# Linear attention block with a gated feed-forward: pairing the transposes of the normalized queries, and the attention product in single PSUM banks

## The chip, the core and the metric
One core of a Trainium2 chip runs the whole program in one launch. The metric is the device time in microseconds (us). In three runs the kernel before took 1098.07, 1098.07 and 1098.23 us, median 1098.07 us. The core has TensorE (PE), which multiplies matrices and writes to PSUM, VectorE (DVE), ScalarE (ACT) and GpSimd (POOL), and a queue of SyncE (SP) that issues all transfers of this kernel. PSUM has eight banks. Every engine works through its own list of instructions in order.

## What is computed
```
xn  = layernorm(x)                            # x: 2048 tokens x 576
qkv = xn @ wqkv                               # 32 heads of 18
phi(t) = where(t > 0, t + 1, exp(t)) + 1e-6
kv  = sum over tokens of phi(k)^T v           # per head
z   = sum over tokens of phi(k)
o   = (phi(q) @ kv) / (phi(q) . z + 1e-6)
s   = o @ wo
g   = silu(gelu(xn @ w1 + b1) @ w2 + b2)      # 576 -> 4608 -> 576
out = x + s * g
```
All in float32; the kernel splits operands into a high and a low part (names ending in h and l) and multiplies high by high, high by low and low by high.

## The kernel before, in words
The 2048 tokens are 16 tiles of 128. A first stage makes keys and values of each tile and sums the state. A second stage, which the change touches, makes the attention output of each tile. A third and much longer stage is the feed-forward network (L1148, L1287, L1403).

At the start of the second stage `fold_wo` multiplies the state by `wo` (L708), so that one 576 x 576 matrix, `kw_h` and `kw_l`, takes normalized queries to s. Then a loop, `for i in range(1, NT + 4)` at L1070, is a pipeline over tiles. Iteration i holds, in this order:

- `query(i)`: 28 matmuls into a pair of banks `pq` (`project`, L313).
- `phi_query(i)`: three passes on ACT (L326, L328, L330) and one on DVE (L332), the last reader of `pq`.
- `transpose_p(i - 2)`: five transposes of the normalized queries of tile i - 2 from `pbuf` into a pair of banks `ptp` (L771), then the high part `th` by ACT (L775) and the low parts `tl` and the end of `th` by DVE (L776, L777).
- `pad(i - 1)`: ACT fills the last columns of `pbuf` (L763).
- `beside(i, 2)`: work for the next stage, in some iterations, on ACT, DVE and SP.
- `normalize(i)`: POOL multiplies by the key sums (L741), more `beside` work, then DVE sums by head (L749 to L753), and POOL writes `pbuf` (L754).
- `attend(i - 4)`: 28 matmuls of `th` and `tl` with `kw` into `ps_s` (L789), a copy to SBUF by ACT (L794) and a store.

From i = 16 on there are no queries; in iterations 17 and 18 `beside` prepares the first weights of the next stage (`z.split`, L486 and L487; `w.hi`, `w.lo`, `w.T`, L859 to L875).

PSUM is shared by two pools. `bank2` hands out three pairs of banks in turn (its pool at L53), `bank1` two single banks in turn (L54). Whoever takes a place in turn waits until the last reader of the tile that held it is done. Before the change `pq`, `ptp` and `ps_s` each take a pair in each iteration, and the single banks serve the transposes and the state of the first stage, `ps_kw` of `fold_wo` and, in the third stage, `a` and `e`.

The whole first and second stages stand under `in_order` (L59): on each engine the instructions run in the order in which this program writes them, and no scheduler moves them. So an instruction that waits holds up everything behind it on its engine.

Of the kernel before, what the change touches and what calls it, by code (L numbers as in the profile page):

```python
# [17 lines left out]
D = 576  # L18
HD = 288
F = 4608  # L20
H = 32
DH = 18
NT = S // P
# [21 lines left out]
def linear_attention_gated_ffn(ctx, tc, x, xT, wqkv, wo, w1, w1e, b1, w2, b2, out):  # L45
    nc = tc.nc
# [31 lines left out]
    def stage(cols, name):  # L78
        t = stg.tile([P, D], F32, tag="stg", name=name)
        return t[:, :cols]  # L80

    def bank2(name):
        return psum.tile([P, 2, 512], F32, tag="pp", name=name)

    def bank1(name):
        return psum1.tile([P, 512], F32, tag="p1", name=name)

    def as2(ap):
        return ap.rearrange("p (a b) -> p a b", a=2)
# [233 lines left out]
    def phi_steps(pool, ps, name, out):  # L323

        e = pool.tile([P, D], F32, tag="e", name=f"e{name}")
        nc.scalar.activation(as2(e), ps[:, :, :HD], AF.Relu, scale=-1.0)  # L326
        yield
        nc.scalar.activation(e, e, AF.Exp, scale=-1.0)  # L328
        yield
        nc.scalar.activation(e, e, AF.Identity, bias=tiny[:, 0:1])  # L330
        r = pool.tile([P, D], F32, tag="phi", name=f"phi{name}")
        nc.vector.scalar_tensor_tensor(  # L332
            as2(r), ps[:, :, :HD], 1.000001, as2(e), op0=ADD, op1=ALU.max
        )
        out += [r, e]
# [177 lines left out]
    def query(t):  # L513
        pq[t] = bank2(f"pq{t}")
        project(t, wq_h, wq_l, pq[t])
# [168 lines left out]
    kw_h = kwp.tile([P, KT, D], F32R, name="kw_h")  # L684
    kw_l = kwp.tile([P, KT, D], F32R, name="kw_l")
    p_bufs = []
    for i in range(2):
        p_bufs.append(t2.tile([P, KT * P], F32, name=f"pbuf{i}", bufs=1))

    krs = []  # L690
# [40 lines left out]
    def split_kw(k, elo):  # L731
        split_w(krs[k], k, kw_h, kw_l, elo)
# [3 lines left out]
    def phi_query(t):  # L736
        phi_q[t] = phi(t2, pq.pop(t), f"q{t}")

    def by_sums(t):
        q_t, e = phi_q[t]  # L740
        nc.gpsimd.tensor_tensor(e, q_t, zb, op=MUL)  # L741

    def normalize(t):
        if t:
            by_sums(t)
            beside(t, 0)
        q_t, e = phi_q.pop(t)
        den = t2.tile([P, 2, H], F32, tag="den", name=f"den{t}")
        nc.vector.tensor_reduce(  # L749
            den[:, 0, :], e.rearrange("p (h d) -> p h d", h=H), axis=mybir.AxisListType.X, op=ADD  # L750
        )
        nc.vector.tensor_scalar_add(den[:, 0, :], den[:, 0, :], 1e-6)
        nc.vector.reciprocal(den[:, 1, :], den[:, 0, :])  # L753
        nc.gpsimd.tensor_tensor(  # L754
            p_bufs[t % 2][:, :D].rearrange("p (h d) -> p h d", h=H),
            q_t.rearrange("p (h d) -> p h d", h=H),
            den[:, 1, :, None].to_broadcast([P, H, DH]),
            op=MUL,
        )

    def pad(t):
        pb = p_bufs[t % 2]
        nc.scalar.copy(pb[:, D:], pb[:, 512:D])  # L763

    pT = {}

    def transpose_p(t):
        pb = p_bufs[t % 2]
        pt = bank2(f"ptp{t}").rearrange("p a b -> p (a b)")
        for k in range(KT):  # L770
            nc.tensor.transpose(pt[:, k * P : (k + 1) * P], pb[:, k * P : (k + 1) * P], ident)  # L771
        th = t2.tile([P, KT, P], F32R, tag="th", name=f"th{t}", bufs=3)
        tl = t2.tile([P, KT - 1, P], F32R, tag="tl", name=f"tl{t}", bufs=3)
        p3 = pt[:, : KT * P].rearrange("p (k c) -> p k c", k=KT)
        nc.scalar.copy(th, p3)  # L775
        nc.vector.tensor_tensor(tl, p3[:, :4, :], th[:, :4, :].bitcast(F32), op=SUB)  # L776
        nc.vector.tensor_tensor(th[64:, 4, :], p3[64:, 4, :], th[64:, 4, :].bitcast(F32), op=SUB)  # L777
        pT[t] = (th, tl)

    def attend(t):  # L780
        th, tl = pT.pop(t)
        ps = bank2(f"ps_s{t}")
        seq = []
        for k in range(4):
            seq += [(th, kw_h, k), (th, kw_l, k), (tl, kw_h, k)]
        seq += [(th, kw_h, 4), (th, kw_l, 4)]
        for i, (st, w, k) in enumerate(seq):
            for h in range(2):
                nc.tensor.matmul(  # L789
                    ps[:, h, :HD], st[:, k, :], w[:, k, h * HD : (h + 1) * HD],  # L790
                    start=(i == 0), stop=(i == len(seq) - 1),
                )
        s_sb = stage(D, f"s{t}")
        nc.scalar.copy(as2(s_sb), ps[:, :, :HD])  # L794
        nc.sync.dma_start(s_dram[t], s_sb)

    def hi_lo(pool, shape, tag, bufs, name):
# [217 lines left out]
    def beside(i, k):  # L1015

        if k == 0:
            if i == 3:
                split_kw(3, nc.vector)
            if i == 4:  # L1020
                xsum[0] = XSums(0, tmp_w1)
            if i == 5:
                xsum[1] = XSums(2, lambda name: as2(kw_pair(name).rearrange("p a d -> p (a d)")[:, :1024]))
            sums(i)
            if i in RESTS:
                half, what, *k = RESTS[i]
                if half not in rests:
                    rests[half] = Rest(half)
                getattr(rests[half], what)(*k)
        else:  # L1030
            if i == 16:
                sums(i)
            if i == 17:
                z = xsum[1]
                z.split(z.u, z.s3, nc.vector)
            if i in SPLITS:
                half, n = SPLITS[i]
                z = xsum[half]
                if i in (8, 12):
                    z.place(not half)  # L1040
                z.split(z.u if n == 3 else z.t, getattr(z, f"s{n}"), nc.vector)
                if not half:
                    spill(i - 8)
            if i == 12:
                w2_raw0.append(load_w2_raw(0))
                w1t[0] = W1(0)
            if i == 13:
                w1t[1] = W1(1)
            if i == 16:
                load_we(0)  # L1050
                z = xsum[1]
                rests["x"] = load_rests(1)
                for n, t in ((2, z.h0), (6, z.tiles[0]), (4, z.h1)):
                    load_rest(1, REST_AT[n], 1, t[:, 4])
            if i == 17:
                w = w1t[0]
                w.hi("a"), w.lo("a")
                for j in (5, 6, 7, 4):
                    w.T(j)
                w.hi(6), w.lo(6)  # L1060
            if i == 18:
                load_we(1)
                w = w1t[0]
                for j in ("c", "d"):
                    w.hi(j), w.lo(j)
# [4 lines left out]
    for i in range(1, NT + 4):  # L1070
        if 1 < i < NT:
            query(i)
        if i in X_STORES:
            at, src = X_STORES[i]
            nc.sync.dma_start(x_dram[:, at : at + src.shape[1]], src.bitcast(F32))
        if i == 1:
            phi_query(0)
            nc.scalar.copy(as2(zb), zb_ps[:, :, :HD])
            by_sums(0)
            groups, made = fold_wo(), []  # L1080
            next(groups)
            steps = phi_steps(t2, pq.pop(1), "q1", made)
            next(steps)
            next(groups)
            next(steps)
            next(groups)
            next(steps, None)
            phi_q[1] = made
            next(groups), next(groups)
            normalize(0)  # L1090
            for _ in groups:
                pass
            pad(0)
        for k in {2: (0, 1), 3: (2,)}.get(i, ()):
            split_kw(k, nc.vector)
        if 1 < i < NT:
            phi_query(i)
        if 2 <= i < NT + 2:
            transpose_p(i - 2)
        if 2 <= i < NT + 1:  # L1100
            pad(i - 1)
        beside(i, 2)
        if i < NT:
            normalize(i)
        if i >= 4:
            attend(i - 4)
# [405 lines left out]
    for step in range(n_chunks):  # L1512
# [3 lines left out]
        h = HOps(c)  # L1516
# [142 lines left out]
```

## Time and profile before
| what | value |
|---|---|
| median of three runs | 1098.07 us |
| the profiled execution | 1098.02 us |
| its span, first to last instruction | 1096.3 us |
| second stage, from the first `query` to the first `a` of the third | about 144.6 to 282.4 us |
| busy share of the span: PE, DVE, ACT, POOL | 99%, 75%, 45%, 43% |

All times in the views are counted from the start of the span. In a timeline row stand the start, the duration, the engine, the line, the operation, what is written from what is read, and in brackets the idle time of the engine just before it with what ended it. In the chain of waits stand the start, the duration and what ran, and the times there are up to 0.2 us later than the starts in the timeline, as it goes by ends. Names are shown without buffer numbers, so `pq` is the queries of any tile.

### The profile page before, as it was taken

The numbers are of one execution on the slowest core, as the hardware profiler recorded it, in microseconds if no ns is written. First come the engines' busy times: TensorE is split into PE (matmuls) and PEld (weight loads), VectorE is DVE, ScalarE is ACT, GpSimd is POOL, SyncE is SP. The second block draws the span as 40 slices with busy tenths as digits, with TensorE's granted clock in tenths as the row PEclk, the third lists the DMA queues.
The fourth block names the chain that finished last, engine by engine and source line by source line (L and its number), as shares of the span: only waits on it lengthen the run. The fifth ranks groups of instructions, "written<-read, shape, count | busy, mean of one in ns | idle before, by whom it ended". The sixth has DMA issues, their size and how long they took to land.

```text
span 1096.3 us, 18084 instructions
## 1 busy us (share of the span) xinstructions
PE 1088.6 (99%) x6702; PEld 1008.5 (92%) x6702; DVE 825.6 (75%) x1132; ACT 490.9 (45%) x844; POOL 472.7 (43%) x403
## 2 busy tenths in 40 slices
PE   9999999999999999999999999999999999999998
PEld 8999989999898998989989989899898998998987
DVE  7785748888798888888888888667476584664856
ACT  6454655555545354454453544524224233242352
POOL 4667444323546446464555553424234143242340
PEclk9999999999999999999999999999999999999999
DMA  7999834675959559486585779978676676766352
GB/s 248 269 262 280 311 135 160 205 242 188 342 214 344 190 211 332 152 317 233 187 330 167 287 239 405 387 249 296 210 245 217 204 236 217 229 222 228 122 181 87
DMA packets 88400, 262.54 MB, mean 239 GB/s; under 512 B 11894, under 2 KB 24182, under 8 KB 85624
## 3 DMA queue, kind: packets, MB, share of 16 engines
q1 hardware_dynamic: 88312, 261.38, 70.1%
q8 instruction: 53, 0.87, 0.3%
q14 instruction: 35, 0.29, 0.1%
HBM read 164.24 MB, written 95.17 MB: 237 GB/s over the span
## 4 chain that ended last, share of the span: by engine, by line
PE 99%; DVE 1%; issue 0%; POOL 0%; ACT 0%; DVEq 0%; POOLq 0%
PE pm L1287 35%; PE a L1148 10%; PE e L1148 10%; PE zy L1148 10%; PE pk L313 6%; PE pq L313 5%; PE ps_s L789 5%; PE b L1148 5%; PE pv L313 4%; PE pd L1403 2%; PE ps_kva L382 1%; PE ptp L771 1%; PE ps_kw L708 1%; PE warm L361 0%; PE ps_kvb L382 0%
## 5 line engine op out<-in xcount | busy, mean ns | idle before, releaser
L1293 DVE TENSOR_TENSOR macc<-pm,macc 128x576 f32<-128x576 f32 x218 | 163.8, 752 | 51.9 <-PE pm L1287 50.3
L813 ACT CAST h_h<-g 128x512 fp32r<-128x512 f32 x204 | 121.7, 621 | 133.9 <-PE pm L1287 132.8
L816 DVE TENSOR_TENSOR h_l<-g,h_h 128x512 fp32r<-128x512 f32 x204 | 161.7, 800 | 0.0
L1253 POOL TENSOR_TENSOR mid<-g 128x512 f32<-128x512 f32 x34 | 44.0, 1293 | 105.4 <-ACT g L1156 105.4
L1247 POOL TENSOR_TENSOR g<-g 128x512 f32<-128x512 f32 x34 | 54.9, 1615 | 49.4 <-DVE h_l L816 28.4
L1156 ACT ACTIVATE g<-b,b1c 128x512 f32<-128x512 f32 x36 | 24.8, 689 | 101.9 <-DVE b L1174 101.9
L1165 ACT COPY mid<-a 128x512 f32<-128x512 f32 x36 | 21.1, 585 | 96.4 <-PE a L1148 96.4
L859 POOL TENSOR_TENSOR w1raw<-w1raw 128x256 f32<-128x256 f32 x18 | 13.3, 737 | 116.7 <-ACT h_h L813 68.2
L1168 DVE TENSOR_TENSOR mid<-b,mid 128x512 f32<-128x512 f32 x36 | 24.8, 690 | 46.3 <-PE b L1148 43.0
L1375 POOL TENSOR_TENSOR fin1l<-fin1h,fin1l 128x288 f32<-128x288 f32 x8 | 6.4, 806 | 119.6 <-DMA fin1l<-s_dram 62.9
L1250 POOL TENSOR_TENSOR g<-g 128x512 f32<-128x512 f32 x34 | 55.2, 1623 | 2.7
L1148 PE MATMUL a<-h0r,wa 128*128 128x512 f32 x144 | 50.4, 390 | 0.0
L1148 PE MATMUL a<-xh,wa 128*128 128x512 f32 x144 | 50.4, 390 | 0.0
L816 DVE TENSOR_TENSOR h_l<-mid,h_h 128x512 fp32r<-128x512 f32 x34 | 48.8, 1437 | 1.2
L1156 ACT ACTIVATE g<-e,b1c 128x512 f32<-128x512 f32 x36 | 24.8, 689 | 51.5 <-DVE e L1181 51.5
L754 POOL TENSOR_TENSOR pbuf<-phiq,den 128x576 f32<-128x576 f32 x16 | 19.4, 1214 | 63.9 <-DVE den L753 63.9
L1244 POOL TENSOR_TENSOR g<-g 128x512 f32<-128x512 f32 x34 | 44.2, 1299 | 2.7
L1181 DVE TENSOR_TENSOR e<-e,mid 128x512 f32<-128x512 f32 x36 | 24.8, 689 | 21.5 <-PE e L1148 21.5
L1171 DVE TENSOR_TENSOR mid<-zy,mid 128x512 f32<-128x512 f32 x36 | 24.9, 691 | 19.5 <-PE zy L1148 19.5
L313 PE MATMUL pk<-wkv_h,xh 128*128 128x288 f32 (+1 forms) x160 | 38.1, 320 | 0.5 <-DVE xh L245 0.5
L313 PE MATMUL pk<-wkv_l,xh 128*128 128x288 f32 (+1 forms) x160 | 38.2, 321 | 0.0
L1174 DVE TENSOR_TENSOR b<-e,mid 128x512 f32<-128x512 f32 x36 | 25.2, 699 | 17.2 <-PE e L1148 16.2
(857 smaller groups left out, 3644.4 us busy)
## 6 DMA issues: line engine op xcount, KB each, us to landing
we<-we_dram SPq DMA_DIRECT2D x36, 448.0 KB
w2raw<-w SPq DMA_DIRECT2D x10, 1152.0 KB
op<-w2o SPq DMA_DIRECT2D x18, 576.0 KB
w1raw<-w SPq DMA_DIRECT2D x18, 512.0 KB
op_a<-wa SPq DMA_DIRECT2D x18, 512.0 KB
op_c<-wc SPq DMA_DIRECT2D x18, 512.0 KB
op_d<-wd SPq DMA_DIRECT2D x18, 512.0 KB
wc<-op_c SPq DMA_DIRECT2D x18, 512.0 KB
```

What stands on the lines that cost most here:

```text
L313: nc.tensor.matmul(ps[:, h, : ws.stop - ws.start], st, w[:, k, ws], start=(begin and i == 0), stop=(end and i == len(seq) - 1), skip_group ...
L789: nc.tensor.matmul(ps[:, h, :HD], st[:, k, :], w[:, k, h * HD : (h + 1) * HD], start=(i == 0), stop=(i == len(seq) - 1),)
L813: nc.scalar.copy(pair[0], src)
L816: eng.tensor_tensor(pair[1], src, pair[0].bitcast(F32), op=SUB)
L1148: nc.tensor.matmul(ps, st, mv, start=first and n == 0, stop=n == len(seq) - 1, skip_group_check=True,)
L1156: nc.scalar.activation(g, ps, AF.Gelu_apprx_tanh, bias=b1c[:, f : f + 1])
L1244: tt(src[5, pr], A(1, 0), A(1, 1), op=ADD)
L1247: tt(src[6, pr], src[5, pr], A(0, 0), op=SUB)
L1250: tt(src[3, pr], A(0, 1), src[6, pr], op=SUB)
L1253: tt(src[7, pr], A(0, 0), A(1, 0), op=SUB)
L1287: nc.tensor.matmul(ps[:, q, :HD], hs[p][st][:, cs], m[:, p, :], start=(n == 0 and i not in CHAIN), stop=(n == 5), skip_group_check=True,)
L1293: nc.vector.tensor_tensor(dst, src, dst, op=ADD)
```

## The change
The transposes move: instead of one tile in every iteration from 2 to 17, two tiles, i - 3 and i - 2, in every odd iteration from 3 to 17. Since a `pbuf` may now be held one iteration longer there are three of them instead of two. The product of `attend` goes into the two single banks, one for each half of the columns, for all tiles but the last, which takes a pair as before. Its copy to SBUF is two copies of 288 columns in place of one of 576.

```diff
-    for i in range(2):
+    for i in range(3):
         p_bufs.append(t2.tile([P, KT * P], F32, name=f"pbuf{i}", bufs=1))
...
-            p_bufs[t % 2][:, :D].rearrange("p (h d) -> p h d", h=H),
+            p_bufs[t % 3][:, :D].rearrange("p (h d) -> p h d", h=H),
...
     def attend(t):
         th, tl = pT.pop(t)
-        ps = bank2(f"ps_s{t}")
+        if t < NT - 1:
+            ps = [bank1(f"ps_s{t}{h}")[:, :HD] for h in range(2)]
+        else:
+
+            both = bank2(f"ps_s{t}")
+            ps = [both[:, h, :HD] for h in range(2)]
...
                 nc.tensor.matmul(
-                    ps[:, h, :HD], st[:, k, :], w[:, k, h * HD : (h + 1) * HD],
+                    ps[h], st[:, k, :], w[:, k, h * HD : (h + 1) * HD],
                     start=(i == 0), stop=(i == len(seq) - 1),
                 )
         s_sb = stage(D, f"s{t}")
-        nc.scalar.copy(as2(s_sb), ps[:, :, :HD])
+        for h in range(2):
+            nc.scalar.copy(s_sb[:, h * HD : (h + 1) * HD], ps[h])
         nc.sync.dma_start(s_dram[t], s_sb)
...
-        if 2 <= i < NT + 2:
-            transpose_p(i - 2)
+        if i % 2 and 3 <= i < NT + 2:
+
+            transpose_p(i - 3), transpose_p(i - 2)
         if 2 <= i < NT + 1:
             pad(i - 1)
```

More of the change, by code (lines that the diff above doesn't have):

```diff
@@ L761, in pad @@
     def pad(t):
-        pb = p_bufs[t % 2]
+        pb = p_bufs[t % 3]
         nc.scalar.copy(pb[:, D:], pb[:, 512:D])
@@ L767, in transpose_p @@
     def transpose_p(t):
-        pb = p_bufs[t % 2]
+        pb = p_bufs[t % 3]
         pt = bank2(f"ptp{t}").rearrange("p a b -> p (a b)")
```

## Prediction
> **What bounds the kernel now.** I read the page first, then busy time by stretch, the waits of PE, and the chain of waits.
>
> ```profile
> PE   9999999999999999999999999999999999999998
> ...
> PEclk9999999999999999999999999999999999999999
> ```
>
> ```profile
> 178.30:258.40 80.10, 80.10 (x612) 80.10 (x611) 66.92 (x95) 42.68 (x71) 27.01 (x22) 1.00 0.60 195
> ...
> 282.40:1096.30 813.90, 808.23 (x4814) 737.63 (x4812) 613.28 (x812) 334.78 (x561) 339.70 (x268) 1.00 0.69 242
> ```
>
> ```profile
> PE warm L361 <- POOL ident masks.py:199: 1.5, 1, 1.5
> PE pk L313 <- DVE xh L245: 0.5, 1, 0.5
> PE e L1148 <- DVE b L1174: 0.3, 1, 0.3
> ```
>
> In the page's 40 slices of 27.4 us PE falls under nine tenths only in the last, and the granted clock is full in all. In a stretch's row the first two numbers are its length and PE's busy time. In the middle of the second stage PE is busy for all of 80.10 us, DVE (third busy figure) for 66.92, ACT for 42.68. The waits of PE (its weight loads aside) are three in the whole span, none in the second stage, and one of 0.3 us in the third. PE is idle for 5.7 of the third stage's 813.90 us, and a last slice of eight tenths holds about 5.5 of that: the tail. So time lost by PE in the second stage is not won back: the third stage starts later by as much and has no idle PE time to absorb it. The question is only whether PE does less work, or waits where it did not.
>
> ```profile
> 1.45 4.53 PE warm L361 x20
> 7.58 3.96 PE pk L313 x28
> ...
> 174.13 0.55 PE ptp L771 x5
> 174.68 3.83 PE ps_s L789 x28
> ...
> 186.51 3.73 PE pq L313 x28
> ...
> 194.52 3.73 PE pq L313 x28
> ...
> 271.41 11.20 PE ps_s L789 x84
> ```
>
> One iteration is 194.52 - 186.51 = 8.01 us: 28 matmuls of 3.73, five transposes, 28 matmuls of `attend` of 3.73 (11.20 / 3), so 0.55 for the transposes.
>
> **Part 1: the transposes in tens.** Work on PE is the same: 80 transposes, 896 matmuls. What could go is the change-over between transposes and matmuls.
>
> ```profile
> 169.50 0.71 PE L771 MATMUL ptp<-ident,pbuf 128*128 128x128 f32 x5
> ```
>
> ```profile
> L771 PE MATMUL ptp<-ident,pbuf 128*128 128x128 f32 x80 | 11.3, 272 | 0.0
> ```
>
> One transpose lasts 0.272, five overlapped 0.71, so they follow each other every (0.71 - 0.27) / 4 = 0.11 us, and five make 0.55: all of the iteration's 0.55. The change-over costs nothing within these roundings (0.01). With eight joints fewer the gain lies between 0 and 0.1 us; I take 0.
>
> **Part 2: the first query after a pair waits.** The pairs of banks go in turn. Before, a round is pq, ptp, ps_s. After, the start runs pq2, pq3, ptp0, ptp1, pq4, with three pairs: pq4 gets the pair of pq3, and must wait until L332 of tile 3 has read it. Before, pq4 got the pair of ptp0.
>
> ```profile
> 169.04 0.67 DVE L776 TENSOR_TENSOR tl<-ptp,th 128x512 fp32r<-128x512 f32 x1
> ...
> 169.26 1.43 POOL L741 TENSOR_TENSOR eq<-phiq,zb 128x576 f32<-128x576 f32 x1 [1.42 <-DVE phiq L332]
> ...
> 169.70 0.65 ACT L326 ACTIVATE eq<-pq 128x576 f32<-128x576 f32 x1 [0.79 <-PE pq L313]
> 169.73 0.29 DVE L777 TENSOR_TENSOR th<-ptp,th 64x128 fp32r<-64x128 f32 x1
> 170.17 0.50 PE L313 MATMUL pq<-wq_h,xh 128*128 128x288 f32 x2
> ...
> 170.73 0.75 DVE L749 TENSOR_REDUCE den<-eq 128x32 f32<-128x576 f32 x1 [0.71 <-POOL eq L741]
> ...
> 171.10 0.78 ACT L330 ACTIVATE eq<-eq,tiny 128x576 f32<-128x576 f32 x1
> ...
> 172.00 0.70 DVE L356 TENSOR_TENSOR kw_l<-kr,kw_h 128x576 fp32r<-128x576 f32 x1
> ...
> 172.73 0.76 DVE L332 SCALAR_TENSOR_TENSOR phiq<-pq,eq 128x576 f32<-128x576 f32 x1
> ```
>
> Before, L777 of tile 0 ends at 170.02 and pq4 starts at 170.17: DVE to PE takes 0.15. After, PE has done the same pieces by then in another order (pq2, pq3, ten transposes), but L332 of tile 3 ends only at 172.73 + 0.76 = 173.49. What sets it is DVE's list: the sum by head waits for POOL (169.26 + 1.43 = 170.69), then come the small steps, the split L356 and L332. DVE's L776 and L777 of tile 0 move behind L332, but they lay in DVE's wait for POOL, so their going frees nothing. So pq4 starts at 173.64, 3.47 later. The 0.10 by which `ps_s` of tile 0 (3.83 against 3.73) was held goes. **Cost 3.4 us.** The lower end is ACT's: pq3 ends 0.55 earlier, so L330 would start at 170.55 and end at 171.33; L332 could not end before 172.1, which leaves 2.1 us.
>
> In later rounds this wait is covered. After a pair, `attend` lies between (1.10 + 3.73 us from one query's end to the next query), and the four passes need 3.1 (L326 starts at 169.70, L330 ends at 171.88, L332 takes 0.76, the hand-over 0.15). In even iterations the next query takes a pair that `ptp` held two iterations ago. A second tile's `ptp` takes the pair of the query before last: no wait. `th` and `tl` of a pair must be ready 7.46 us (an attend and a query) after the transposes; two tiles need twice 0.69 on ACT (L775, below) and twice 0.96 on DVE (L776, L777) behind L332, which ends 2.9 after the query and so 1.8 after the transposes: ready after some 3.7. DVE's work is unchanged, 84% of the stretch. The third `pbuf` keeps POOL's L754 from waiting. SP's list is the same, its stores of s a little later.
>
> **Part 3: attend in two single banks.** Each attend now takes both, so the next must wait for both copies by ACT. With a query between, that has 3.73 us: covered. Where attends stand together it has nothing: tiles 11 and 12, 13 and 14 (ten transposes lie between 12 and 13; tile 15 has a pair).
>
> ```profile
> L715 ACT COPY kw<-ps_kw 126x288 f32<-126x288 f32 x4 | 1.6, 401 | 0.7 <-PE ps_kw L708 0.7
> ```
>
> ```profile
> 266.25 1.72 DVE L483 TENSOR_TENSOR xt<-xh,xt 128x1024 f32<-128x1024 f32 x1
> 266.42 0.71 PE L771 MATMUL ptp<-ident,pbuf 128*128 128x128 f32 x5
> 266.62 0.64 ACT L794 COPY s<-ps_s 128x576 f32<-128x576 f32 x1 [1.38 <-PE ps_s L789]
> ...
> 267.17 0.69 ACT L775 CAST th<-ptp 128x640 fp32r<-128x640 f32 x1
> ```
>
> A copy of half the columns is taken as 0.40, the row of L715. Before, the copy starts 0.20 after PE could go on (266.62 against 266.42); the first half is ready one matmul (0.13) earlier, so at 0.07. ACT's rows overlap by 0.1 (267.17 against 267.26), so the second half runs from 0.37 to 0.77, and PE's first matmul into its bank starts at 0.92 in place of 0.13. **Tile 12: 0.8 us.** Between 12 and 13 the 1.10 of the transposes covers 0.92.
>
> For tile 14 ACT isn't free. Its list has, ahead of the copies of tile 13, the splits of the next stage:
>
> ```profile
> 270.29 1.36 DVE L483 TENSOR_TENSOR xt<-xl,xt 128x1024 f32<-128x1024 f32 x1
> ...
> 271.58 1.21 DVE L483 TENSOR_TENSOR xu<-xu,xl 128x1024 f32<-128x1024 f32 x1
> ...
> 272.82 1.05 ACT L486 CAST xh<-xu 128x1024 fp32r<-128x1024 f32 x1 [0.68 <-DVE xu L483]
> ...
> 273.90 1.23 DVE L487 TENSOR_TENSOR xl<-xu,xh 128x1024 fp32r<-128x1024 f32 x1
> ...
> 276.18 0.69 DVE L875 TENSOR_TENSOR wa<-w1raw,wa 128x512 fp32r<-128x512 f32 x1
> ...
> 276.95 0.74 POOL L859 TENSOR_TENSOR w1raw<-w1raw 128x256 f32<-128x256 f32 x1 [6.37 <-DVE wa L875]
> ...
> 278.53 0.41 ACT L870 CAST w<-w1t 128x256 fp32r<-128x256 f32 x1 [3.19 <-POOL w1t L862]
> ...
> 278.84 0.63 ACT L794 COPY s<-ps_s 128x576 f32<-128x576 f32 x1
> ```
>
> Read down from the third row: ACT splits xu, DVE makes its low part, then that of the first weights, POOL makes two differences of weights, ACT splits the second, and only then copies tile 13. From the first to the copy: 278.84 - 272.82 = 6.02 us. Before, that copy was late too (attend 13 had ended by 275.2, a third into the chain's row of 84 matmuls), but nobody needed its pair yet. After, with E the moment PE is done with attend 12: copies of tile 12 at E + 0.07 and 0.37, two `th` (now together) at 0.67 and 1.27, the split of xu at 1.87 (DVE has xu ready: see below), the copy of tile 13 at 1.87 + 6.02, plus 0.4 since DVE must put two tiles' `tl` ahead of the low part instead of one: E + 8.3. DVE's list from L332 of tile 15 to xu is two tiles' 0.96, 1.72, the sums by head with 1.3, 1.36 and 1.21, in all 7.5 us; L332 ends 3.0 after query 15, E lies 1.10 + 3.73 + 0.8 + 3.73 = 9.4 after it, so xu is ready at E + 1.1, before 1.87. PE's first matmul into the second bank follows at 8.3 + 0.3 + 0.40 + 0.15 = E + 9.15. Without a wait it would start at 1.10 + 3.73 + 0.13 = E + 4.96. **Tile 14: 4.2 us**, between 3.8 (without the 0.4) and 4.5.
>
> A rule of the Trainium skill speaks to these gaps. No wait of PE in the trace before is over 1.5 us, and the granted clock is full in every slice. The start shows the slow clock: 20 transposes in 4.53 us, 0.23 each against 0.11, until pk at 7.58 runs at the full pace. "TensorE: Matmul & The Clock Gate" (Part 1) says that the clock falls to half after an idle window of about 3.4 us, a window that runs freely. By that rule the gaps ahead of pq4 and tile 14 (3.3 to 4 us) are at the edge; the trace before can neither show nor exclude it.
>
> **Sum.** 3.4 + 0.8 + 4.2 = 8.4 us, against the profiled execution of 1098.02 (0.05 below the median, 1.7 above its span): **1106.4 us**. The operands of the third stage are ready earlier relative to PE, but it has no wait to lose.
>
> **Rivals.**
> - The clock falls in one of the two long gaps. At the start the slow stretch lasts from 1.45 to 7.58, 6.1 us, which at half pace loses 3.1; half as long a stretch loses 1.6. 1108.0 to 1109.5 us. For it: both gaps are far longer than any in the trace. Against it: each is short of the 6.1 us. The rule of the Trainium skill above is this one.
> - The gaps are at their lower ends: DVE reaches L332 as soon as ACT allows, and the chain to tile 13's copy isn't lengthened: 2.1 + 0.8 + 3.8 gives 1104.7. For it: DVE's order leaves some slack. Against: the rows ahead of L332 stay as they were.
> - Not slower: the banks come free in time, because pq4 does not get pq3's pair and tile 14 not tile 13's banks. It decides if L332 of tile 3 ends by 169.9 or the copies of tile 13 within 1.1 us of its attend. Then only the 0.1 of tile 0 and up to 0.1 of the joints go: 1097.8. Against: three pairs and two banks in turn leave no other place.
> - The change doesn't do what it says: the ten transposes don't run together, since the second tile waits for L332 of tile 2. That ends before 169.26, when POOL takes it up; the second five start at 169.5. No wait, no cost.
>
> **Chances.** Forecast 0.70, clock 0.14, lower ends 0.12, not slower 0.04 (the last rival is part of none). The range takes in the first three: 1104.7 to 1109.5. A measurement of this kernel tells about 0.2%, 2.2 us, from no change: faster 0.01, same 0.03, slower 0.96.
>
> **What would show it.** Right: PE idle ahead of pq4 until about 173.6, ended by DVE's L332; no wait from there to the last query; a wait of 0.8 ahead of `ps_s` of tile 12 and of 4.2 ahead of tile 14, both ended by ACT's copies; the third stage about 8.4 later and equally long. Wrong: cycles of transposes shorter than 1.10 for ten, waits inside the steady rounds (DVE late with `tl`), transposes at 0.2 us each, or a third stage of another length.

## The result and the profile after

| what | before | after |
|---|---|---|
| median | 1098.09 us (four executions, 1098.07 to 1098.23) | 1111.14 us (four executions: 1108.64, 1111.74, 1111.57, 1110.72) |
| profiled execution | 1098.02 us | 1108.64 us, the shortest of the four |
| its span | 1096.3 us | 1106.9 us |

The ratio is 1.0114, with a 95% interval of 1.0102 to 1.0127: slower by 13 us. The forecast was 1106.4 us, and the range ended at 1109.5. So the direction was as forecast, and the time lies above the range.

First the page of the changed kernel, its 40 slices (27.7 us each):

```profile
PE   9999998999899999999999999999999999999998
...
PEclk9999999999899999999999999999999999999999
```

PE now has two slices under nine tenths besides the last. The seventh (166 to 194 us) holds the first rounds of the second stage with transposes, the eleventh (277 to 304 us) the end of the stage. And in the eleventh the granted clock isn't full: before, it was in every slice.

The waits of PE in the changed kernel (total in us, times, longest):

```profile
PE ps_s L794 <- ACT s L800: 4.5, 2, 4.2
PE pq L313 <- DVE phiq L332: 3.2, 1, 3.2
```

Two rows, three waits, with the releasers that the forecast named. The timeline shows each. The lines of the changed kernel are shifted: the product L789 is now L794, the copy L794 is L800, and the weight splits L859 to L875 are L865 to L881. These are rows of PE and DVE from the start, then of PE and ACT from the end:

```profile
168.81 0.74 DVE L332 SCALAR_TENSOR_TENSOR phiq<-pq,eq 128x576 f32<-128x576 f32 x1
169.40 1.25 PE L771 MATMUL ptp<-ident,pbuf 128*128 128x128 f32 x10
173.03 0.74 DVE L332 SCALAR_TENSOR_TENSOR phiq<-pq,eq 128x576 f32<-128x576 f32 x1
173.82 0.53 PE L313 MATMUL pq<-wq_h,xh 128*128 128x288 f32 x2 [3.17 <-DVE phiq L332]
...
270.45 0.70 PE L794 MATMUL ps_s<-kw_h,th 128*128 128x288 f32 x2 [0.36 <-ACT s L800]
...
276.80 1.09 ACT L486 CAST xh<-xu 128x1024 fp32r<-128x1024 f32 x1
...
283.07 0.40 ACT L876 CAST w<-w1t 128x256 fp32r<-128x256 f32 x1 [3.72 <-POOL w1t L868]
283.38 0.69 ACT L800 COPY s<-ps_s 128x288 f32<-128x288 f32 x2
283.83 0.91 PE L794 MATMUL ps_s<-kw_h,th 128*128 128x288 f32 x2 [4.17 <-ACT s L800]
285.01 0.68 PE L794 MATMUL ps_s<-kw_h,tl 128*128 128x288 f32 x2
285.49 0.68 PE L794 MATMUL ps_s<-kw_h,th 128*128 128x288 f32 x2
...
289.19 0.43 PE L794 MATMUL ps_s<-kw_h,th 128*128 128x288 f32 x2
289.45 0.43 PE L794 MATMUL ps_s<-kw_l,th 128*128 128x288 f32 x2
```

The ten transposes run without a wait (L332 of tile 2 ends at 169.55, before the second five of them), and then PE stands still until L332 of tile 3 ends at 173.77. At the end, the copies of tile 13 stand behind the splits in ACT's list, from 276.80 to 283.38, which is 6.58 us. The last four rows show what the forecast did not have: a pair of matmuls takes 0.48 us (285.49 - 285.01) ahead of 288.4, and 0.26 (289.45 - 289.19) behind it. After its wait PE works at half pace.

The steady rounds in the chain of waits of the changed kernel, from one ten of transposes to the next (between them lie two products and two queries):

```profile
185.27 1.09 PE ptp L771 x10
...
201.27 1.09 PE ptp L771 x10
```

Two iterations last 201.27 - 185.27 = 16.00 us against 2 x 8.01 before, PE without a gap. Nothing is won in them beyond 0.02 us, and nothing is lost.

Last, PE's busy time and the granted clock by stretch of the changed kernel. In a row stand the stretch, its length, PE's busy time (with its instructions), the granted clock, and the share and rate of DMA:

```profile
161.72:293.46 131.74, 124.04 (x922) 0.97 0.60 198
```

```profile
168.93:172.35 3.42, 1.72 (x15) 1.00 0.82 246
172.35:175.76 3.41, 1.94 (x14) 1.00 0.47 195
...
278.16:281.57 3.41, 1.50 (x12) 1.00 0.78 277
281.57:284.98 3.41, 1.15 (x4) 0.50 0.41 167
284.98:288.40 3.42, 3.42 (x16) 0.50 0.99 340
288.40:291.81 3.41, 3.41 (x27) 1.00 0.77 308
293.40:1106.90 813.50, 808.22 (x4814) 1.00 0.68 240
```

The first row runs from the third query to the first `a` of the third stage. Before, the same stretch (161.28 to 282.45) was 121.17 us long and PE was busy for all of it. So 10.57 us are added: 131.74 - 124.04 = 7.70 of idle time, and 124.04 - 121.17 = 2.87 in which PE counts as busy but is late. Of these about 1.9 are the slow clock (18 matmuls at 0.24 in place of 0.133), and the other 0.9 or so mainly matmuls held for the second bank of a tile. For tile 12 that is 0.27: its first two pairs of matmuls start 0.54 us apart (270.45 and 270.99) in place of 0.27. The third stage is as long as before (813.50 against 813.90), as forecast. Around the changed stage, the profiled execution lost time to the clock at the end only. The three others are 2.1 to 3.1 us longer, with a mean granted clock of 0.993 or 0.994 against its 0.996.

### The profile page after: what moved, and what is told of

Same layout as the page of the kernel before. It is cut to its first block, busy times and chain, and to the rows that moved or that the text cites. A ratio compares the mean times of both kernels' runs of the same rounds, so it can differ in the third digit from the quotient of the medians.

```text
span 1106.9 us, 18091 instructions
## 1 busy us (share of the span) xinstructions
PE 1091.3 (99%) x6702; PEld 1010.1 (91%) x6702; DVE 826.5 (75%) x1132; ACT 492.2 (44%) x860; POOL 474.0 (43%) x403
## 4 chain that ended last, share of the span: by engine, by line
PE 95%; DMA 2%; DVE 2%; POOL 1%; ACT 1%; issue 0%; SPq 0%; DVEq 0%; POOLq 0%; ACTq 0%
PE pm L1294 34%; PE a L1155 10%; PE e L1155 10%; PE zy L1155 10%; PE pk L313 6%; PE b L1155 5%; PE pq L313 5%; PE ps_s L794 5%; PE pv L313 4%; PE pd L1410 2%; PE ps_kva L382 1%; DMA x<-x 1%; DMA w1u<-w1e 1%; PE ptp L771 0%; DMA w<-wqkv 0%; PE ps_kw L708 0%
## 5 line engine op out<-in xcount | busy, mean ns | idle before, releaser
L865 POOL TENSOR_TENSOR w1raw<-w1raw 128x256 f32<-128x256 f32 x18 | 13.2, 735 | 124.2 <-ACT h_h L819 68.1
L794 PE MATMUL ps_s<-kw_h,th 128*128 128x288 f32 x160 | 36.3, 308 | 4.5 <-ACT s L800 4.5
```

The source lines that it names most:

```text
L794: nc.tensor.matmul(ps[h], st[:, k, :], w[:, k, h * HD : (h + 1) * HD], start=(i == 0), stop=(i == len(seq) - 1),)
```

## The experiments

Two theories were to be told apart after this result. The first: the three waits cost the forecast 8.4 us, and the rest, some 4 us, is the clock falling at **both** long gaps. The rival: the rest is more waiting (a step that is later than reckoned), or a cost of the new order itself, in the transposes or in the doubled copies.

### One half of the change at a time

`single_only` has the product in single banks, with the transposes one tile at a time as before:

```diff
-        if i % 2 and 3 <= i < NT + 2:
-            transpose_p(i - 3), transpose_p(i - 2)
+        if 2 <= i < NT + 2:
+            transpose_p(i - 2)
```

> Attend in the two single banks as changed; the transposes one tile per iteration as before. Theory of waits: with pq and ptp alone taking pairs in turn, pq4 gets the pair of ptp0 as before, so nothing is lost at the start. At the end attends 12 and 13 have five transposes (0.55 us) between them and the attend before, so each waits 0.92 - 0.13 - 0.55 = 0.25; attend 14 waits for the late copy of tile 13, about 4.4. 1098.1 + 4.9 = 1103.0, and about 2 more (1105) if the clock falls in that gap. Rival, that the transposes in tens cost the time: 1098 to 1100 here.

Measured: 1104.02 us (1103.97 to 1104.73) beside 1098.56, ratio 1.0051 (1.0036 to 1.0066). One wait is left of the three; its row among the waits of PE in `single_only`:

```profile
PE ps_s L794 <- ACT s L800: 3.6, 1, 3.6
```

It is the one ahead of tile 14, shorter than the 4.4 expected, and 3.41 us at a granted clock of 0.50 follow it. Waits ahead of tiles 12 and 13, expected with 0.25 each, are not among the rows. The 3.6 us of wait and up to 1.7 of slow clock make 5.3 of the 5.5 us.

`tens_only` has the transposes in tens, with every product in a pair of banks as before:

```diff
-        if t < NT - 1:
+        if t < 0:
             ps = [bank1(f"ps_s{t}{h}")[:, :HD] for h in range(2)]
```

> Transposes in tens as changed; attend in pairs of banks for all tiles as before. Theory of waits: pairs in turn give pq4 the pair of pq3 (3.2 us lost, and up to 2 more by the clock), and in each odd iteration from 5 to 15 attend gets the pair of the query just ahead of the transposes, whose last reader needs 3.1 us while the transposes give 1.1: 2.0 us in each of six. No wait at the end. 1098.1 + 3.2 + 12 = 1113.3, up to 1115.5 with the clock. Rival, that the single banks cost the time and the tens are free: 1098 to 1103.

Measured: 1122.27 us (1121.55 to 1122.63) beside 1098.56, ratio 1.0217 (1.0200 to 1.0234): 7 us above the top of what was expected. The waits of PE in `tens_only` are the expected ones:

```profile
PE ps_s L794 <- DVE phiq L332: 11.8, 6, 2.0
PE pq L313 <- DVE phiq L332: 3.2, 1, 3.2
```

So the tens need the single banks: with three pairs in turn and two of them taken by the tens, every second `attend` waits 2.0 us for L332. The waits add to 15.0, but 23.7 us were lost. The stretches of `tens_only` show where the others went:

```profile
169.07:172.49 3.42, 1.38 (x13) 1.00 0.79 225
172.49:175.90 3.41, 2.28 (x9) 0.50 0.56 235
175.90:179.31 3.41, 3.41 (x17) 0.50 0.00 0
...
186.14:189.55 3.41, 2.54 (x21) 1.00 0.20 77
189.55:192.97 3.42, 2.33 (x17) 1.00 0.41 114
...
206.62:210.03 3.41, 1.45 (x11) 1.00 0.01 2
210.03:213.44 3.41, 3.41 (x16) 0.50 0.00 0
...
227.10:230.51 3.41, 1.86 (x14) 1.00 0.67 183
...
244.17:247.58 3.41, 1.45 (x12) 1.00 0.57 223
247.58:250.99 3.41, 3.41 (x16) 0.50 0.41 171
...
264.64:268.06 3.42, 1.46 (x11) 1.00 0.08 32
268.06:271.47 3.41, 3.41 (x17) 0.50 0.00 0
```

The stretches were cut so that the halved ones begin at 172.49, 210.03, 247.58 and 268.06. These lie 11, 11 and 6 times 3.41 us apart: the clock is set anew on a grid of 3.41 us that runs through. A wait of 2.0 us that lies whole in one cell of the grid (busy 1.45 or 1.46) is followed by a cell at half clock, and such a cell, when PE is busy throughout, does a little over half the work: 16 or 17 matmuls in place of 27 (the row 288.40:291.81 above). The same wait split over two cells (busy 2.54 and 2.33) halves nothing, and neither does the one that leaves 1.86 busy. In the five halved cells PE is busy for 15.9 us, and half of that, 8.0, is lost. The profiled execution of 1121.55 lost 23.0, about the 15.0 of the waits and these 8.0.

### Each end by itself

`tail_pairs` is the changed kernel with the last four products in pairs as before:

```diff
-        if t < NT - 1:
+        if t < NT - 4:
```

> As changed, but attends 12 to 15, which have no query ahead of them, take pairs. Theory of waits: the waits ahead of tiles 12 and 14 go, and the clock stays up at the end; left is the wait ahead of pq4. 1098.1 + 3.1 = 1101.2, or up to 1103.5 if the clock falls in that gap. Rival, that single banks or copies in halves cost a little with every tile: nearer to 1109.

Measured: 1103.92 us (1102.24 to 1104.59) beside 1098.56, ratio 1.0046 (1.0032 to 1.0061), above the 1101.2 expected with the start's wait alone, and 0.4 above the 1103.5 expected with a slow clock behind it. The two waits by ACT are gone; the start's is still there with 3.2, and a new one stands in the list of `tail_pairs`:

```profile
PE ptp L771 <- POOL pbuf L754: 0.5, 1, 0.5
```

The last ten transposes now come before `pbuf` of tile 15 is written, as no wait for the copies of tile 11 holds them back: a wait that the removed one had covered. The clock is the rest. In the profiled execution (1104.58) the cell of the start's wait, from 171.22 to 174.63, has PE busy for 0.23 us, and the next one runs at half clock. The execution of 1102.24 has a mean granted clock of 0.999, the three of 1103.27 and more 0.996 or 0.997.

`start_single` is the changed kernel with tiles 0 and 1 transposed singly, as before, and tens from iteration 5 on:

```diff
-        if i % 2 and 3 <= i < NT + 2:
+        if i in (2, 3):
+            transpose_p(i - 2)
+        if i % 2 and 5 <= i < NT + 2:
```

> As changed, but the first two tiles are transposed one by one as before, and tens begin with tiles 2 and 3. Theory of waits: pq4 gets the pair of ptp0 again, and the 3.2 us at the start and its clock loss go. Left are tile 12 with 0.8 and tile 14 with 4.3: 1098.1 - 0.1 + 5.1 = 1103.1, 1105 with the clock down at the end. Rival, that tens cost in every round: over 1106.

Measured: 1105.52 us (1104.90 to 1105.85) beside 1098.56, ratio 1.0063 (1.0048 to 1.0078), half a microsecond above the 1105 expected with a slow clock. Among PE's waits the one for L332 is gone, the two for ACT are unchanged at 4.5 in all, and two cells are at half pace behind tile 14's.

### The gaps filled

This tells the theories apart. `busy_both` is the changed kernel with 27 transposes of the identity ahead of `pq` of tile 4 and 36 ahead of the product of tile 14, into banks that are free then; nobody reads what they write. PE has something to do, but it waits for the same releasers.

```diff
+    def busy(ps, n):
+        for _ in range(n):
+            nc.tensor.transpose(ps[:, :P], ident, ident)
...
+        if t == 14:
+            busy(bank2("busy14")[:, 0], 36)
...
+        if i == 4:
+            busy(bank1("busy4"), 27)
```

> As changed, plus transposes of the identity that nobody reads, on PE inside the two long waits: 27 ahead of pq4 (2.9 us) and 36 ahead of attend 14 (3.9 us). The waits stay as long, only PE is busy in them. If the waits cost what the trace shows (3.1 at the start, 0.8 and 4.3 at the end) and the rest of the 13 us is the clock: 1098.2 + 8.1 = 1106.3 in every run, with a spread under 0.5 us and the granted clock at 1.000. Rival, that the rest is not the clock but something else in the changed kernel: 1110 to 1112 as changed. Rival, that the added work delays what is behind it: more than as changed.

Measured: 1106.71 us (1106.45 to 1107.32) beside 1098.11, ratio 1.0081 (1.0065 to 1.0096). With more work on PE the kernel is **4.4 us faster** than the changed one, and the spread of its executions falls from 3.1 to 0.9 (under 0.5 was expected). PE still waits for the same releasers at both gaps, but only briefly, so the added work does not outlast the gaps:

```profile
PE ps_s L800 <- ACT s L806: 0.6, 2, 0.4
...
PE pq L313 <- DVE phiq L332: 0.2, 1, 0.2
```

Around the two gaps `busy_both` shows a full clock:

```profile
161.00:179.00 18.00, 17.76 (x137) 1.00 0.53 181
274.00:294.00 20.00, 19.76 (x146) 1.00 0.75 275
```

So the waits themselves cost 1106.71 - 1098.11 = 8.6 us, and what the changed kernel has above that, 1111.14 - 1106.71 = 4.4, is the clock. The rival (more waiting, or a cost of the order) would have left the time at 1111.

`busy_start` fills only the first gap, `busy_tail` only the second.

> As changed, plus only the 27 transposes ahead of pq4. Clock theory: it stays up at the start and falls at the end, 1106.3 + 2 = 1108.3. If the clock isn't the cause: 1110 to 1112.

> As changed, plus only the 36 transposes ahead of attend 14. Clock theory: it stays up at the end; the wait of 3.2 us ahead of pq4 may or may not bring it down, by where its windows of 3.4 us lie: 1106.3 where it doesn't, up to 1109.0 where it does (5.7 us at half pace with 28 matmuls of a query cost 2.6 with the attends in pairs). If the clock isn't the cause: 1110 to 1112.

Measured: 1108.01 us (1107.60 to 1108.24) and 1107.97 us (1106.89 to 1110.07), ratios 1.0090 (1.0076 to 1.0104) and 1.0093 (1.0079 to 1.0106). With only the end's gap open the clock costs 1.3 us (one cell at half pace in the profile). With only the start's gap open it varies from one execution to the next: the two executions with a mean granted clock of 1.000 took 1106.89 and 1107.18, one of 0.998 took 1108.75, one of 0.996 took 1110.07. The two medians add to 2.6 us of clock, not 4.4. Where the gaps lie on the grid differs from kernel to kernel, so the amounts need not add; that they differ for this reason alone is argued, not shown.

### Is it the two banks, or ACT's list?

`copy_first` is the changed kernel with one step moved: in iteration 17 the product of tile 13 and its copies are written ahead of the next stage's splits.

```diff
+        if i == 17:
+            attend(i - 4)
         beside(i, 2)
...
-        if i >= 4:
+        if i >= 4 and i != 17:
             attend(i - 4)
```

> Only the place of one step in iteration 17 differs from the changed kernel: attend of tile 13, with its two copies on ACT, is written ahead of the work for the next stage instead of behind it. If ACT's list makes the long wait of tile 14 (theory), the copies of tile 13 no longer stand behind the weight splits, tile 14 waits 0.8 us like tile 12 instead of 4.2, and no slow clock follows there: 1098.1 + 3.2 + 0.8 + 0.8 = 1102.9, up to 1104.5 in executions whose clock falls after the wait ahead of pq4. If two banks in place of three pairs make it whatever ACT's order is (rival), the wait of tile 14 stays near 4.2 and the time near 1111.

Measured: 1106.83 us (1105.61 to 1110.41) beside 1099.43, ratio 1.0061 (1.0030 to 1.0091). That is above the 1104.5 expected; 1.3 us of it is the time of the kernel before, which is higher here. On this chip the executions scattered more, those of before too (1098.17 to 1105.53). In the profiled execution of `copy_first` some of the time is lost in the first stage, where PE waits once for 2.3 us and 3.41 us at half clock follow. So the trace is read from the third query on, as above. PE's waits in `copy_first`, and ACT's timeline:

```profile
PE ps_s L794 <- ACT s L800: 0.7, 2, 0.4
...
PE a L1157 <- ACT s L800: 0.5, 1, 0.5
```

```profile
284.85 0.70 ACT L800 COPY s<-ps_s 128x288 f32<-128x288 f32 x2 [2.63 <-PE ps_s L794]
285.43 1.06 ACT L486 CAST xh<-xu 128x1024 fp32r<-128x1024 f32 x1
```

The copies come ahead of the splits, and tile 14 waits as little as tile 12 (0.4 for the first bank, about 0.8 with the second). So of the 4.2 us two banks in turn make only the 0.8, and ACT's list makes the rest. It takes both: with the splits first in ACT's list but pairs of banks (`tail_pairs`), there is no wait at all. The missed part is a wait of 0.5 ahead of the first `a` of the third stage, which takes a bank of tile 14 whose copies now stand behind the splits. And the start's gap halved the clock in this profile:

```profile
174.85:178.26 3.41, 0.69 (x5) 1.00 0.82 323
178.26:181.67 3.41, 3.41 (x16) 0.50 0.00 0
```

### The change without its waits

`both` joins `start_single` and `tail_pairs`: no wait of the three is left.

> Transposes in tens from tiles 2 and 3 on, the first two one by one; attends 12 to 15 in pairs, the others in single banks. Theory of waits: all three waits go and the clock stays up; left is the gain of the joints, 16.000 against 16.014 us for two iterations in the traces, five times 0.014, and the 0.1 ahead of attend 0: 0.2 faster than before, 1098.0 beside 1098.2, within 0.1%. Rival, that tens or single banks cost anything in the steady rounds: slower than before by over 0.5 us.

Measured: 1099.35 us (1098.91 to 1100.10, eleven executions) beside 1098.11, ratio 1.0011 (1.0003 to 1.0020): 1.2 us slower than before, not 0.2 faster. From the third query to the first `a` the profiled execution takes 122.15 us (161.62 to 283.77) against 121.17 before, so 1.0 lies in this stage. It is lost at the last ten transposes, in the timeline of `both`:

```profile
270.37 0.71 PE L771 MATMUL ptp<-ident,pbuf 128*128 128x128 f32 x5
271.59 0.77 PE L771 MATMUL ptp<-ident,pbuf 128*128 128x128 f32 x5 [0.51 <-POOL pbuf L754]
```

The second five start 1.22 us after the first, in place of 0.55: they wait for `pbuf` of tile 15. The product behind them starts at 272.46, 0.87 after the second five; in the kernel before it is 0.47 (271.17 - 270.70). The next step was to transpose the last two tiles singly too, which leaves tens and single banks to the steady rounds alone (`mid_only`):

```diff
-        if i in (2, 3):
+        if i in (2, 3, NT, NT + 1):
             transpose_p(i - 2)
-        if i % 2 and 5 <= i < NT + 2:
+        if i % 2 and 5 <= i < NT:
```

> The changed kernel with all that waits taken out of it: tiles 0, 1, 14 and 15 are transposed singly as before, attends 12 to 15 go into pairs as before; tens and single banks stay for the steady rounds, tiles 2 to 13. Theory: the 1.05 us that the kernel with only the start single and the end in pairs lost around its last ten transposes go, no wait is left, the clock stays full, and the steady rounds win 0.01 us each: 1098.2 beside 1098.1, within 0.5 us of before. Rival (the pairing itself has a cost in the steady rounds that the waits hid): 1099 or more.

Measured: 1100.06 us (1098.39 to 1106.07, twelve executions) beside 1099.43 on the chip that scattered, ratio 1.0005 (0.9989 to 1.0022): no difference that can be told from before. The time is 0.6 us above that of before, and the interval holds both the 0.1 expected and the 0.9 of the rival, so the trace has to decide. From the third query to the first `a`, in `mid_only` and then in the kernel before:

```profile
163.02:284.08 121.06, 121.06 (x922) 1.00 0.62 201
```

```profile
161.28:282.45 121.17, 121.17 (x923) 1.00 0.62 201
```

No wait is left, the clock is full, and the stretch is 0.11 us shorter. Of that, 0.07 comes from the product of tile 0, which is held no longer (from its start to the next query 3.73 us against 3.80), and 0.04 is left for six tens. That is all that the idea of the change is worth on PE, 0.01% of the time. No version here is shown to beat the kernel before.

## Why the prediction was wrong

**What held.** PE bounded the stage, and its lost time was given on whole to the end (third stage 813.50 against 813.90 us). Pairing saves nothing in the steady rounds (0.02 in two iterations). No wait stands in them. The three waits have the places and the releasers that were named:

| term | predicted | measured | from |
|---|---|---|---|
| ahead of `pq` of tile 4 | 3.4 us | 3.2 | idle 3.17 in the timeline |
| ahead of `ps_s` of tile 12 | 0.8 | 0.8 | 0.36 idle, the rest for the second bank |
| ahead of `ps_s` of tile 14 | 4.2 | 4.2; some 4.6 with the second bank and with tile 13 (below) | 4.17 idle; 8.6 less the two above |
| the three together | 8.4 | 8.6 | `busy_both` |

ACT's way from the split of xu to the copy was 6.58 us against 6.02 + 0.4 predicted. That the sum comes so near is in part luck: the start was 0.2 cheaper than reckoned and the end 0.4 dearer. The prediction has the copies of tile 12 start 0.07 us after PE is done with the tile, and tile 13 lose nothing. In ACT's timeline of the changed kernel the copies stand behind the fill of `pbuf`, which waits for POOL:

```profile
274.90 0.24 ACT L763 COPY pbuf<-pbuf 128x64 f32<-128x64 f32 x1 [4.20 <-POOL pbuf L754]
275.05 0.69 ACT L800 COPY s<-ps_s 128x288 f32<-128x288 f32 x2
```

They start 0.59 after PE (which begins the next transposes at 274.46), and the product of tile 13 loses 0.27 at its second bank: its first two pairs of matmuls start 0.54 us apart, as those of tile 12 do. Had the clock stayed up, 1106.4 would have been within 0.3 us of the time.

**What failed** is the step from the waits to the time. The sum, 3.4 + 0.8 + 4.2, has no term for the clock, and the runs show one of 4.4 us. The clock stood only in the first rival, "The clock falls in one of the two long gaps", with a chance of 0.14, and against it stood "each is short of the 6.1 us" of the slow start. Three things were wrong in that.

- The size of the gap that is needed. The 6.1 us of the start say how long the clock stayed slow there, not how long PE must idle before it falls. In the traces, a cell of 3.41 us at full clock in which PE was busy for 0.23 us (`tail_pairs`) to 1.50 us (the changed kernel) was followed by one at half clock, and a cell at full clock with 1.72 busy or more was not (the tail of the kernel, where PE's work is over, is left out of this). So two microseconds of waiting are enough if they lie in one cell. By that rule a wait of 4.2 us always brings the clock down: even cut in the middle it leaves each of two cells idle for 2.1 us and busy for 1.3. A wait of 3.2 us escapes only if the grid cuts it nearly in the middle. That is what happened in the profiled execution (1.72 and 1.94 busy), and, to go by their mean clocks, not in the three others.
- The number of gaps. By that rule the end's gap always brings the clock down, and the start's does so too unless the grid cuts it in the middle. A fall in both was not among the rivals, and the range ended below it.
- The price. One halved cell costs up to 1.7 us, and two can follow each other: a cell that begins slow and still holds part of the wait is followed by another (281.57 to 288.40 after the change, 172.49 to 179.31 in `tens_only`). The profiled execution lost 1.9 at the end; 1098.09 + 8.6 + 1.9 = 1108.6 is its time. The median lies 2.5 above that. Where a profile caught one halved cell at the start (`copy_first`), the query of tile 4 took 5.52 us in the chain in place of 4.00, so 1.5; with two cells, as in `tens_only`, it took 6.52, so 2.5.

The Trainium skill, "TensorE: Matmul & The Clock Gate" (Part 1), has the right mechanism: half or full clock, set on a window of about 3.4 us that runs freely. The traces agree with that (3.41 us, clock 0.50). It asks for an idle window, and the prediction read that as a gap as long as the window; by the runs, a window in which PE is idle for 56% is idle enough, and one idle for 50% isn't.

What stays open: whether the three longer executions of the changed kernel really lost their 2.1 to 3.1 us at the start, as only the shortest has a trace; and why the two single fillings add to less than both. The scatter points to the start: with only the start's gap open (`busy_tail`) they spread over 3.2 us, those of the changed kernel over 3.1, and with the start's gap filled (`busy_start`) over 0.6.

## What to carry to other kernels

Price a new wait on TensorE with the clock that follows it: here a wait that left 56% or more of a 3.41 us cell idle cost up to 1.7 us more per halved cell, and 8.6 us of waits became 13. Where tiles take buffers in turn, write down for every place who had it before, and then look at what stands ahead of that reader in its engine's list: the same two banks cost 0.8 us behind an idle ACT and 4.2 behind one with other work written first. And ask of a regrouping whether the joints that it saves cost anything at all: the steady row before (0.55 us for five transposes, 0.11 each) said that they were free, and the version without waits is only 0.11 us shorter in this stage.

## What the runs showed of the hardware

- In these traces the clock is granted in cells of 3.41 us on a grid that runs through the execution. Before the kernel's tail, a cell at full clock in which PE was busy for 44% or less (1.50 us, the changed kernel) is followed by one at half clock, and one with 50% or more (1.72 us) by a full one; what happens between them no run shows. From half clock it takes more: a cell busy for 2.28 us (67%, `tens_only`) was followed by another at half clock, and cells busy throughout by a full one.
- Pairs of 128x288 matmuls follow each other at 0.48 us at half clock, against 0.27 at full clock.
- Transposes of the identity count as work for the clock: with them in the two gaps it stayed full (`busy_both`).
- More work can be faster: 63 transposes that nobody reads, put into two waits, took 4.4 us off the time.
